# Interleaving the end of each superblock and splitting the first x load in a fused convolution and two-matmul kernel

## The chip, the cores and the metric

One core of a Trainium2 chip. The metric is the device time of one execution in microseconds (us), the median of several. A profiled execution has a span from its first to its last instruction, 1.8 to 2.2 us shorter than its time. Lengths and starts below are read from one profiled execution of each kernel, times from several.

## The reference

A dynamic convolution: each of 32768 tokens (8 sequences of 4096) has 8 heads with 7 softmax weights each, and each head's 24 channels are the weighted sum of that token and the 6 before it. The result x (192 wide) goes through two matmuls with a shrinking function between them.

```python
w = softmax(weight_gen)                       # [B, S, 8 heads, 7 taps]
x_pad = concat([zeros(B, 6, 192), x], axis=1) # six "halo" rows in front
out = einsum('bshk,bskhg->bshg', w, windows_of_7(x_pad))
h = out.reshape(32768, 192) @ w_in            # 192 -> 2048
y = (h - tanh(h)) @ w_out                     # 2048 -> 192, float32
```

## The kernel before

Tokens are worked in 32 superblocks of 1024 (128 partitions of 8 tokens). Four engines form a pipeline over different superblocks:

- GpSimd (POOL) makes the 7 products x times weight of superblock n+2 (`even`, `odd`, `last`); a DMA adds half of them to the other half.
- TensorE (PE) transposes and sums the products of n+1 by matmuls against an identity (`pc`), in two pieces; ScalarE (ACT) copies them out as `convT`.
- TensorE makes the 16 f tiles of n (`ph`, 128 rows of w_in's 2048 columns each); ScalarE takes their tanh; VectorE (DVE) subtracts (`gt`).
- TensorE makes the 8 output blocks of n−1 (`obank`), ScalarE copies them out.

The kernel's use of PSUM (where its matmuls write) is three buffers of two banks, used in turn by f tiles and transpose pieces, and two output banks.

```python
psum_h = tile_pool(name="psum_h", bufs=3, space=PSUM)     # "ph" and "pc" in turn
obank = [psum_o.tile([P, 512], FP32, ...) for i in range(2)]

def gemm1(n, f):                    # one f tile
    ph = psum_h.tile([P, 2, HT], FP32, name="ph", tag="ph")
    ...                             # 6 matmuls of 512 columns, two row halves side by side
    last_act[0] = nc.scalar.activation(out=th[:], in_=ph_f, func=ACT.Tanh)
    last_sub[0] = nc.vector.tensor_sub(gt[:], ph_f, th[:])

def gemm2(i):                       # output block i, 16 steps of two matmuls
    for f in range(NFT):
        for r, n, j, po in ops: nc.tensor.matmul(po[:, 0:D], lhsT=g_of[n][f][...], rhs=w_out[...])
    ...
    last_act[0] = nc.scalar.activation(out=out_sb[:, j, :], in_=po[:, 0:D], func=ACT.Copy)

for n in range(NTOT):
    ...                             # loads of n + 3
    for p in range(J):              # J = 8
        gemm1(n, 2 * p)
        gemm1(n, 2 * p + 1)
        ...
        if n >= 1:
            gemm2((n - 1) * J + p)
        ...
        if n + 1 < NTOT:            # after block 6: both transpose pieces (n > 1)
            if p == (6 if n > 0 else 7): conv(n + 1, (0, 1))
            if p == (6 if n > 1 else 7): conv(n + 1, (2,))
        if p == 6 and n + 3 < NTOT:
            softmax_norm(n + 3)     # sum and reciprocal, VectorE
```

x is loaded with its halo, 14 rows per partition of which 8 are its own.

The softmax here doesn't subtract the row's maximum and nothing guards it: scores larger than these inputs give would overflow.

## Time and profile before

| | before |
|---|---|
| time | 770.2 us (770.0 to 770.4) |
| span of the profiled execution | 768.7 us |
| TensorE busy | 96% |
| first f tile starts | 20.73 us |
| superblock 0 (VectorE's), first f tile to first f tile | 23.41 us |
| superblocks 1 to 3, together | 74.0 us |
| superblocks 4 to 30, most of them, each | 22.63 us |

In the timeline a line is: start, busy time, engine, source line, operation, what it writes and reads, count; in brackets the idle time before it and what ended it. The ends of matmuls are modelled, so TensorE's row can look unbroken where it waits 0.2 us: compare starts with the length that the same group has elsewhere. In the waits, a row is the waiter, what it waited for, the sum in us, the number of times, the longest. The prediction below shows the lines.

### The profile page before, as it was taken

How to read it: one execution, taken by the hardware profiler on the slowest of the kernel's cores; microseconds unless marked ns; L12 is line 12 of the kernel's file. 1: busy time of each engine (PE TensorE's matmuls, PEld its weight loads, DVE VectorE, ACT ScalarE, POOL GpSimd, SP SyncE). 2: the span in 40 equal slices, each digit the busy share in tenths (PEclk: the TensorE clock that was granted, in tenths of full speed). 3: DMA queues.
4: the chain of work that ended last, by engine and by line, in shares of the span. 5: the costliest groups of instructions: out<-in, count | busy, mean ns of one | idle time of the engine just before them, and what ended most of it. 6: DMA issues, size and time to landing. Idle time of an engine off the chain costs nothing.

```text
span 768.7 us, 32330 instructions
## 1 busy us (share of the span) xinstructions
PE 736.7 (96%) x14784; PEld 583.1 (76%) x14784; DVE 652.9 (85%) x595; ACT 640.8 (83%) x865; POOL 695.2 (90%) x290
## 2 busy tenths in 40 slices
PE   2799999999999999999999999999999999999997
PEld 2377787777777777788777777777778777787777
DVE  5987888888898888889888888888888988888883
ACT  1777878888888888888888888888888888888883
POOL 5999999999999999999999999999999999999100
PEclk9999999999999999999999999999999999999999
DMA  7823776555677555577655557765556765542412
GB/s 209 184 81 87 182 181 150 118 145 147 169 182 174 131 129 148 150 180 182 164 123 133 150 160 182 180 128 137 143 150 172 182 181 115 125 142 72 98 43 84
DMA packets 25847, 111.37 MB, mean 145 GB/s; under 512 B 4800, under 2 KB 9456, under 8 KB 21624
## 3 DMA queue, kind: packets, MB, share of 16 engines
q1 hardware_dynamic: 14688, 76.95, 29.9%
q0 software_dynamic: 10816, 31.99, 25.8%
q8 instruction: 115, 1.88, 1.0%
q10 hardware_dynamic: 208, 0.39, 0.2%
q14 instruction: 20, 0.16, 0.1%
HBM read 54.49 MB, written 25.17 MB: 104 GB/s over the span
## 4 chain that ended last, share of the span: by engine, by line
PE 93%; DVE 2%; issue 1%; POOL 1%; DMA 1%; ACT 1%; SPq 0%; POOLq 0%
PE ph L257 43%; PE obank L289 43%; PE pc L233 6%; DVE gt L269 2%; PE po L323 1%; DMA x_t<-in_x_dram 1%; POOL even L192 1%; ACT th L267 0%; ACT convT L244 0%; POOL odd L192 0%; DVE zr L151 0%; DVE zsum L145 0%; SPq L117 0%; SPq L93 0%; SPq L121 0%
## 5 line engine op out<-in xcount | busy, mean ns | idle before, releaser
L269 DVE TENSOR_TENSOR gt<-ph,th 128x1024 bf16<-128x1024 f32 x512 | 602.8, 1219 | 93.3 <-ACT th L267 92.7
L267 ACT ACTIVATE th<-ph 128x1024 f32<-128x1024 f32 x512 | 497.2, 1022 | 65.7 <-PE ph L257 64.9
L257 PE MATMUL ph<-convT,w_in 64*128 64x512 bf16 x3072 | 382.1, 378 | 7.5 <-DVE gt L269 5.0
L289 PEld LDWEIGHTS <-gt 64*128 64x128 bf16 x7936 | 345.1, 94 | 53.4 <-issue 2.5
L289 PE MATMUL obank<-w_out,gt 64*128 64x192 bf16 x7936 | 374.6, 243 | 2.9 <-issue 2.1
L192 POOL TENSOR_TENSOR even<-x_t,wsm 128x1536 bf16<-128x1536 f32 x94 | 272.8, 2903 | 3.9 <-DMA x_t<-in_x_dram 1.6
L192 POOL TENSOR_TENSOR odd<-x_t,wsm 128x1536 bf16<-128x1536 f32 x93 | 269.9, 2903 | 0.0
L257 PEld LDWEIGHTS <-w_in 64*128 64x128 bf16 x3072 | 180.1, 94 | 108.4 <-issue 11.8
L192 POOL TENSOR_TENSOR last<-x_t,wsm 128x1536 bf16<-128x1536 f32 x31 | 103.4, 3336 | 0.0
L307 ACT ACTIVATE out_sb<-obank 128x192 f32<-128x192 f32 x248 | 81.9, 330 | 10.5 <-PE obank L289 4.6
L244 ACT ACTIVATE convT<-pc 128x1024 bf16<-128x1024 f32 x64 | 48.9, 808 | 31.6 <-PE pc L233 31.5
L233 PE MATMUL pc<-ident,even 64*128 64x64 bf16 x2304 | 47.9, 192 | 2.9 <-POOL even L192 1.5
L233 PEld LDWEIGHTS <-even 64*128 64x128 bf16 x2304 | 42.7, 96 | 4.1 <-issue 2.2
L201 POOL DMA_DIRECT2D even<-odd x29 | 34.9, 1205 | 9.1 <-POOL odd L192 9.1
L163 POOL TENSOR_TENSOR wsm<-e_t,zr 128x448 f32<-128x448 f32 x30 | 41.7, 1390 | 0.0
L233 PE MATMUL pc<-ident,odd 64*128 64x64 bf16 x448 | 15.5, 198 | 13.1 <-DVE odd L192 12.8
L135 ACT ACTIVATE e_t<-wg_t 128x448 f32<-128x448 f32 x32 | 18.5, 578 | 8.2 <-DMA wg_t<-in_weight_gen_dram 8.2
L233 PE MATMUL pc<-ident,last 64*128 64x64 bf16 x768 | 23.3, 192 | 1.8 <-issue 1.7
L145 DVE TENSOR_REDUCE zsum<-e_t 128x64 f32<-128x448 f32 x32 | 19.5, 609 | 2.9 <-ACT e_t L135 2.9
L233 PEld LDWEIGHTS <-odd 64*128 64x128 bf16 x448 | 11.3, 100 | 13.6 <-DVE odd L192 12.9
L151 DVE RECIPROCAL zr<-zsum 128x64 f32<-128x64 f32 x30 | 16.6, 553 | 3.0
L233 PEld LDWEIGHTS <-last 64*128 64x128 bf16 x768 | 17.0, 96 | 2.2 <-issue 1.8
(20 smaller groups left out, 48.7 us busy)
## 6 DMA issues: line engine op xcount, KB each, us to landing
x_t<-in_x_dram SPq DMA_DIRECT2D x24, 1344.0 KB
even<-odd POOLq DMA_DIRECT2D x29, 1024.0 KB, 8.8
out_dram<-out_sb SPq DMA_DIRECT2D x31, 768.0 KB
x_t<-in_x_dram SPq DMA_DIRECT2D x8, 1176.0 KB
wg_t<-in_weight_gen_dram SPq DMA_DIRECT2D x32, 224.0 KB
x_t<-in_x_dram SPq DMA_DIRECT2D x8, 157.5 KB
w_in<-in_moe_w_in_dram POOLq DMA_DIRECT2D x6, 128.0 KB, 7.5
w_out<-in_moe_w_out_dram POOLq DMA_DIRECT2D x1, 768.0 KB, 10.8
```

What stands on the lines that cost most here:

```text
L135: nc.scalar.activation(out=e_t[:].rearrange("p j h k -> p (j h k)"), in_=wg_t[:].rearrange("p j h k -> p (j h k)"), func=ACT.Exp,)
L145: nc.vector.reduce_sum(out=zsum[:], in_=e_t[:].rearrange("p j h k -> p (j h) k"), axis=AX.X)
L163: return eng.tensor_mul(wsm.rearrange("p j h k -> p (j h) k"), e_t[:].rearrange("p j h k -> p (j h) k"), zr.rearrange("p (n o) -> p n o", ...
L192: eng.tensor_mul(dst[k].rearrange("p c j h g -> p j h c g"), x_t[:, k : k + J, :].rearrange("p j (h c g) -> p j h c g", h=H, c=NC), w[:, : ...
L201: nc.gpsimd.dma_start(out=even[:].rearrange("p i c j h g -> p (i c j h g)")[:, 0:ACC], in_=odd[:].rearrange("p i c j h g -> p (i c j h g)" ...
L233: nc.tensor.matmul(pc[:, r, col : col + R], lhsT=prods[c][gi][r * R : (r + 1) * R, c, 2 * j : 2 * j + 2].rearrange("p j h g -> p (j h g)") ...
L244: nc.scalar.activation(out=convT[:, c0 : c0 + nch, :].rearrange("p c (j r t) -> p r (c j) t", r=2, t=R), in_=pc[:, :, 0 : nch * JH * R].re ...
L257: nc.tensor.matmul(ph[:, r, :], lhsT=w_in[r * R : (r + 1) * R, c, f * P : (f + 1) * P], rhs=convT[r * R : (r + 1) * R, c, :], start=(c == ...
L267: last_act[0] = nc.scalar.activation(out=th[:], in_=ph_f, func=ACT.Tanh)
L269: last_sub[0] = nc.vector.tensor_sub(gt[:], ph_f, th[:])
L289: mm = nc.tensor.matmul(po[:, 0:D], lhsT=g_of[n][f][r * R : (r + 1) * R, col : col + P], rhs=w_out[r * R : (r + 1) * R, f, :], start=(r == ...
L307: last_act[0] = nc.scalar.activation(out=out_sb[:, j, :], in_=po[:, 0:D], func=ACT.Copy)
```

## The change

Its intent: spread the ends of superblocks so that TensorE alternates between kinds of work while ScalarE and VectorE catch up, and start the first products on the part of x that needs no halo.

```diff
-        if s == 0:
+        if n == 0:
+            rows(0, P, HALO, HALO + J)      # first tile: own rows, all partitions
+            rows(16, P, 0, HALO)            # then the halo
+            rows(1, 16, 0, HALO)
+            no_halo()
+        elif s == 0:
 ...
-    FA = 8 * P                              # first part of w_in
+    FA = 7 * P
 ...
     products(
         0,
-        on_vector=(3, 4, 5, 6),
-        sums=(3, 0, 4, 5, 1, 6, 2),
+        on_vector=(6, 3, 4, 5),
+        order_of=(6, 0, 3, 1, 4, 5, 2),
+        sums=(6, 3, 0, 4, 5, 1, 2),
 ...
+        spread = 1 < n < NTOT - 1
-        for p in range(J):
+        for p in range(J - 1 if spread else J):
 ...                                         # (superblock 1: pieces after blocks 5 and 6)
+        if spread:
+            (pc,) = conv_sums(n + 1, (0, 1))
+            conv_out(n + 1, pc, (0, 1), 0, 1)
+            if n + 3 < NTOT:
+                softmax_norm(n + 3)
+            gemm1(n, NFT - 2)
+            conv_out(n + 1, pc, (0, 1), 1, 1)
+            gemm2((n - 1) * J + J - 1, 0)   # steps 0 to 7 of the block
+            (pc,) = conv_sums(n + 1, (2,))
+            conv_out(n + 1, pc, (2,))
+            gemm2((n - 1) * J + J - 1, 1)   # steps 8 to 15
+            gemm1(n, NFT - 1)
```

The lines are shortened ("..."), with comments added. The rest of the diff splits `conv` into `conv_sums` and `conv_out` and lets `gemm2` run by halves.

More of the change, by code (lines that the diff above doesn't have):

```diff
@@ L103, in load_x, with rows @@
         x_t = xpool.tile([P, HALO + J, D], FP32, name="x_t")
-        def rows(p0, p1):
-            win = x[b, s0 + p0 * J - HALO : s0 + p0 * J - HALO + 1]
+        def rows(p0, p1, r0=0, r1=HALO + J):
+            win = x[b, s0 + p0 * J - HALO + r0 : s0 + p0 * J - HALO + r0 + 1]
             nc.sync.dma_start(
-                out=x_t[p0:p1, :, :],
+                out=x_t[p0:p1, r0:r1, :],
                 in_=bass.AP(
@@ L111, in rows, with no_halo @@
                     offset=win.offset,
-                    ap=[[J * D, p1 - p0], [D, HALO + J], [1, D]],
+                    ap=[[J * D, p1 - p0], [D, r1 - r0], [1, D]],
                 ),
             )
-        if s == 0:
+        def no_halo():
             nc.sync.dma_start(
@@ L120, in load_x @@
             )
-            nc.sync.dma_start(
-                out=x_t[0:1, HALO : HALO + J, :],
-                in_=x[b, 0:J].rearrange("(p j) d -> p j d", p=1),
-            )
+        if n == 0:
[4 more added lines that the diff above has]
+        elif s == 0:
+            no_halo()
+            rows(0, 1, HALO, HALO + J)
             rows(1, 16)
@@ L167, in scale, with products @@
         )
-    def products(n, on_vector=(), sums=None, hooks={}, behind=None):
+    def products(n, on_vector=(), order_of=None, sums=None, hooks={}, behind=None):
         x_t = x_of.pop(n)
@@ L189, in products @@
             hooks[-1]()
-        for k in range(K):
+        for k in order_of or range(K):
             eng, w = (nc.vector, wsm_v) if k in on_vector else (nc.gpsimd, wsm[:])
@@ L215, in products, with conv_sums @@
             prods_of[n] = [[dst[k] for k in (sums or range(K))]] * NC
-    def conv(n, *parts):
+    def conv_sums(n, *parts):
         prods = prods_of[n]
@@ L221, in conv @@
             conv_of[n] = cpool.tile([P, NC, HT], BF16, name="convT")
-        convT = conv_of[n]
         pcs = [psum_h.tile([P, 2, HT], FP32, name="pc", tag="ph") for _ in parts]
@@ L241, in conv, with conv_out @@
                             )
-        for chunks, pc in zip(parts, pcs):
-            c0, nch = chunks[0], len(chunks)
-            nc.scalar.activation(
-                out=convT[:, c0 : c0 + nch, :].rearrange("p c (j r t) -> p r (c j) t", r=2, t=R),
-                in_=pc[:, :, 0 : nch * JH * R].rearrange("p r (cj t) -> p r cj t", t=R),
-                func=ACT.Copy,
-            )
         if parts[-1][-1] == NC - 1:
             prods_of.pop(n)
+        return pcs
+    def conv_out(n, pc, chunks, c0=None, nch=None):
+        c0 = chunks[0] if c0 is None else c0
+        nch = len(chunks) if nch is None else nch
+        col = (c0 - chunks[0]) * HT // 2
+        nc.scalar.activation(
+            out=conv_of[n][:, c0 : c0 + nch, :].rearrange("p c (j r t) -> p r (c j) t", r=2, t=R),
+            in_=pc[:, :, col : col + nch * JH * R].rearrange("p r (cj t) -> p r cj t", t=R),
+            func=ACT.Copy,
+        )
+    def conv(n, *parts):
+        for pc, chunks in zip(conv_sums(n, *parts), parts):
+            conv_out(n, pc, chunks)
     def gemm1(n, f):
@@ L266, in gemm1 @@
         g1_act[0] = last_act.get(0)
+        gt = gpool.tile([P, TOK], BF16, name=f"gt{f}", tag=f"gt{f}")
         last_act[0] = nc.scalar.activation(out=th[:], in_=ph_f, func=ACT.Tanh)
-        gt = gpool.tile([P, TOK], BF16, name=f"gt{f}", tag=f"gt{f}")
         last_sub[0] = nc.vector.tensor_sub(gt[:], ph_f, th[:])
@@ L274, with gemm2 @@
     out_of = {}
-    def gemm2(i):
+    def gemm2(i, half_of=None):
         ops = []
@@ L282, in gemm2 @@
             n, j = divmod(blk, J)
-            if r == 0:
+            if r == 0 and half_of != 1:
                 half[blk] = obank[blk % 2]
             ops.append((r, n, j, half[blk]))
-        for f in range(NFT):
+        f0, f1 = (0, NFT) if half_of is None else (half_of * J, half_of * J + J)
+        for f in range(f0, f1):
             for r, n, j, po in ops:
@@ L299, in gemm2 @@
                     order(mm, g1_act[0] if i == 1 else last_act[0], "row tiles in one bank")
-        if i > 0:
+        if i > 0 and half_of != 0:
             blk = i - 1
@@ L360, in load_w_in @@
                 in_=bass.AP(
-                    tensor=src.tensor, offset=src.offset, ap=[[G * F, H], [F, GC], [1, f1 - f0]]
+                    tensor=src.tensor,
+                    offset=src.offset,
+                    ap=[[G * F, H], [F, GC], [1, f1 - f0]],
                 ),
@@ L409 @@
                 products(n + 2, behind=last_sub[0] if n > 1 else None)
-            if n + 1 < NTOT:
-                if p == (6 if n > 0 else 7):
-                    conv(n + 1, (0, 1))
-                if p == (6 if n > 1 else 7):
-                    conv(n + 1, (2,))
+            if n == 0 and p == 7:
+                conv(1, (0, 1))
+                conv(1, (2,))
+            if n == 1 and p == 5:
+                conv(2, (0, 1))
+            if n == 1 and p == 6:
+                conv(2, (2,))
             if n == 0 and p == 2:
@@ L417 @@
                 products(2)
-            if p == 6 and n + 3 < NTOT:
+            if n <= 1 and p == 6:
                 softmax_norm(n + 3)
+        if spread:
[10 more added lines that the diff above has]
+            gemm1(n, NFT - 1)
     gemm2(LAST)
```

## The prediction

> **What bounds the kernel now.** I read the page's busy shares first, then the chain of waits, then the timeline of one late superblock (a block of 1024 tokens; there are 32), because a share of busy time is an average and the change touches only the ends of superblocks and the first load. TensorE is at 96%, and the chain is TensorE almost throughout:
>
> ```profile
> PE 736.7 (96%) x14784; PEld 583.1 (76%) x14784; DVE 652.9 (85%) x595; ACT 640.8 (83%) x865; POOL 695.2 (90%) x290
> ...
> PE 93%; DVE 2%; issue 1%; POOL 1%; DMA 1%; ACT 1%; SPq 0%; POOLq 0%
> ```
>
> So only TensorE's own instruction time or a gap in it can move the total. The timeline around the end of superblock 24 (first superblock = 0) shows both:
>
> ```profile
> 590.61 2.36 DVE L269 TENSOR_TENSOR gt<-ph,th 128x1024 bf16<-128x1024 f32 x2 [0.26 <-ACT th L267]
> ...
> 591.31 0.88 PE L233 MATMUL pc<-ident,even 64*128 64x64 bf16 x48
> ...
> 592.01 0.41 PE L233 MATMUL pc<-ident,last 64*128 64x64 bf16 x16
> ...
> 592.24 0.53 PE L233 MATMUL pc<-ident,even 64*128 64x64 bf16 x24
> ...
> 592.46 1.51 ACT L244 ACTIVATE convT<-pc 128x1024 bf16<-128x1024 f32 x2 [0.60 <-PE pc L233]
> ...
> 592.71 0.30 PE L233 MATMUL pc<-ident,odd 64*128 64x64 bf16 x8
> ...
> 593.02 1.47 PE L257 MATMUL ph<-convT,w_in 64*128 64x512 bf16 x12
> ...
> 593.88 1.94 ACT L267 ACTIVATE th<-ph 128x1024 f32<-128x1024 f32 x2
> ...
> 594.31 1.50 PE L289 MATMUL obank<-w_out,gt 64*128 64x192 bf16 x32
> ...
> 594.94 2.36 DVE L269 TENSOR_TENSOR gt<-ph,th 128x1024 bf16<-128x1024 f32 x2 [0.79 <-ACT th L267]
> ...
> 595.63 1.48 PE L257 MATMUL ph<-convT,w_in 64*128 64x512 bf16 x12
> ```
>
> Read the starts, not the modelled ends. A pair of f tiles takes 594.31 − 593.02 = 1.295 us (0.648 a tile), an output block 1.32, the pair of both 2.615. The transposes take 592.01 − 591.31 = 0.70 us for 48, so 14.7 ns each, and all 104 should take 1.53. But the next f tile starts 1.71 after them. The 0.18 us in between is a hidden wait: f tile 14 takes the buffer of tile 13 (three PSUM buffers in turn, two of them taken by the transpose pieces). DVE's pair starts at 590.61 and the second of the two ends at 592.97, and 593.02 is 0.05 later. A superblock is 8 × 2.615 + 1.71 = 22.63 us, and the starts of the late superblocks are 22.62 to 22.64 apart.
>
> TensorE's other gaps between 44 and 753 us, in the view of waits:
>
> ```profile
> PE pc L233 <- issue: 2.8, 5, 1.7
> PE obank L289 <- issue: 2.1, 2, 1.3
> PE ph L257 <- issue: 0.8, 1, 0.8
> ```
>
> They are 5.7 us without a releaser, most of it near transposes in superblocks 1 to 3 and 20. Each of the four largest ends 1.3 to 1.6 us after one 16 KB packet of the instruction queue ended, so I read them as late instruction fetch; that is an inference. The head, in the timeline:
>
> ```profile
> 6.84 1.92 POOL L358 DMA_DIRECT2D w_in<-in_moe_w_in_dram  x3 [5.53 <-DVE wsm L163]
> 10.28 1.75 DVE L192 TENSOR_TENSOR odd<-x_t,obank 128x1536 bf16<-128x1536 f32 x1 [3.77 <-DMA x_t<-in_x_dram]
> 10.32 2.90 POOL L192 TENSOR_TENSOR even<-x_t,wsm 128x1536 bf16<-128x1536 f32 x1 [1.57 <-DMA x_t<-in_x_dram]
> ...
> 16.05 2.89 POOL L192 TENSOR_TENSOR even<-x_t,wsm 128x1536 bf16<-128x1536 f32 x1
> ...
> 20.73 4.85 PE L257 MATMUL ph<-convT,w_in 64*128 64x512 bf16 x24 [0.91 <-ACT convT L244]
> 20.85 3.39 PEld L257 LDWEIGHTS <-w_in 64*128 64x128 bf16 x18 [1.14 <-DMA w_in<-w_in]
> ```
>
> The weights are ready at 6.5, x comes only at 10.3; the first f tile waits for the transposes (which wait for GpSimd's third product, 16.05 + 2.89 = 18.94) and, at nearly the same moment, for the copy of w_in.
>
> [...]
>
> **The change part by part.**
>
> *TensorE's order at the end of superblocks 2 to 30.* No matmul is added or removed. Before: transposes (two pieces), tiles 14, 15, block. After: piece 1, tile 14, half a block, piece 2, other half, tile 15, and then the next superblock's tiles 0 and 1 directly. Durations, besides those above: piece 1 is 64 matmuls, 0.94 us, piece 2 is 40, 0.59, half a block 0.66. Latencies: f tile start to tanh 0.86 (593.88 − 593.02); tanh to its subtraction 1.05 when DVE is free (596.50 to 597.55); tanh to tanh 0.92; subtraction to subtraction 1.13 when queued (superblock 0); subtraction 1.22, and the buffer is refilled 0.05 after it (13 of 13 such tiles of superblock 0). Copy of one chunk 0.60, next ScalarE start 0.50 later; block end to its output copy 0.22. Time 0 is the start of piece 1; buffers in turn A (12), B (13), C (piece 1), A (14), B (piece 2), C (15), A (0'), B (1'), C (2'), A (3').
>
> - Tile 14 runs 0.94 to 1.59 and no longer waits for 13: the 0.18 is saved. Half block to 2.25, piece 2 to 2.84, half block to 3.50.
> - ScalarE: first copy 1.15, tanh 14 at 1.80, second copy 2.72 to 3.32, third 3.22, output 3.72. C is free at 3.37, so tile 15 runs 3.50 to 4.15: just in time.
> - DVE: subtraction 13 ends 1.65, the softmax pair at 2.84, subtraction 14 2.85 to 4.07. A is free at 4.12, tile 0' runs 4.15 to 4.80: just in time. 1' to 5.44.
> - tanh 15 at 3.50 + 0.86 = 4.36, subtraction 15 at 5.41 to 6.63. Subtraction 0' follows at 6.54 and ends 7.76.
> - The next block needs tile 15 in its last weight loads, near 6.5 to 6.7: about 0.1 late, ends 6.86. Tile 2' to 7.51. Tile 3' needs A: 7.76 + 0.05 = 7.81. It starts 0.30 late.
>
> Counted from tile 15: TensorE has three tiles, a block and one tile before 3', 4 × 0.648 + 1.32 = 3.91 us, while the chain to 3' is 0.86 + 1.05 + 1.13 + 1.22 + 0.05 = 4.31. So 0.40 us of new wait, whichever of the two places shows it, against 0.18 saved: +0.22 a superblock, 22.85 instead of 22.63. Over 29 superblocks: +6.4 us. ScalarE's third copy (0.3 us more) lies in its slack.
>
> *Superblock 1.* Piece 1 moves one pair earlier; GpSimd's products for it end at 57.24, before it. I put +0.1.
>
> *Head.* Main x is 128 × 6144 B = 0.79 MB of 1.38 MB. Before, x flowed from about 3.4 to 9.4 us, some 228 GB/s. The main transfer is now issued at about 1.2, ahead of the zero row's 0.83 us issue, and should serve VectorE's tap 6 (the product for the 7th and last filter position, which reads no halo row) at about 7.1. But taps 3 and 0 need the halo; the bytes are the same, so these start only as much earlier as the transfer does: 9.6 instead of 10.3. GpSimd still does three taps (8.6 us) and ends at about 18.2; VectorE gains more, but nothing waits for that. w_in's first part is 7/8 as large, so its copy, 18.4 to 20.5 before, is ready at about 19.8. First f tile 0.8 us earlier. The second part of w_in is larger and needed one tile sooner: it may stall tile 7 by a microsecond, yet DVE's softmax pair at 30.5 to 31.7 lies there and hides it. Superblock 0 is DVE's (16 subtractions at 1.13 and two softmax pairs), so the 0.8 is kept.
>
> *Instruction gaps.* The transposes, the densest stretch of instructions, are spread, but 252 of them still pass in 2.84 us. The loads that share the DMA engines in superblocks 1 to 3 remain. I allow −1.5 of 5.7.
>
> Sum: −0.8 + 0.1 + 6.4 − 1.5 = +4.2, from 770.2 to 774.4. The wait of 0.40 is read from margins of 0.03 to 0.13 us, and a late tile 0' would overlap it, not add; so I shade to 773.
>
> **The rivals.** (1) The order works as intended: no wait replaces the 0.18, the instruction gaps go. Then −5.2 − 5 − 1, about 759. For it: three of the waits come out just in time in my table; against it: the 4.31 us chain is made of durations that barely vary. GpSimd would also limit it: its own period is 22.64 to 22.65 us, with 7 us of slack at the last transposes (its last add lands at 720.3, they start at 727.1). (2) The margins fail: ScalarE's second copy delays tile 15 and subtraction 14 delays 0', by another 0.3 us each superblock; about 782. (3) The order is neutral, the saved wait equals the new one, and only the head and some gaps show: 768. (4) The second part of w_in comes later than the softmax pair hides: +1, the head's gain gone: 774.
>
> **Range and chances.** 2% is 15.4 us. Rival 1, the best case, is short of that, rival 2 as well. So 773, 8 in 10 within 765 to 782; faster by over 2%: 0.01, within 2%: 0.96, slower by over 2%: 0.03.
>
> **What would show it.** Late superblocks 22.85 us apart (right) or 22.45 to 22.65 (rival 1). Tile 14 right behind piece 1, 0.94 us after it began; the second pair's second tile of a superblock starting 0.05 us after the end of subtraction 0', about 0.3 late. VectorE's first product at 7.1, GpSimd's at 9.6, the first f tile at 19.9. The step most likely wrong is the 0.40, then the instruction gaps, which I can't derive.

The instruction queue carried 115 packets and 1.88 MB, 16 KB each, by the page of the kernel before.

## The result

| | before | after |
|---|---|---|
| time, median of 4 | 770.24 us | 774.38 us (773.71 to 774.72) |
| span of the profiled execution | 768.73 | 772.52 |
| first f tile starts | 20.73 | 19.18 |
| superblock 0 | 23.41 | 23.30 |
| superblock 1 | 25.55 | 28.70 |
| superblocks 2 and 3, together | 48.47 | 46.45 |
| superblocks 4 to 30, the most common length | 22.63 | 22.85 |
| superblocks 4 to 30, together | 613.25 | 617.14 |

The ratio is 1.0053, with a 95% interval of 1.0036 to 1.0070. A ratio is the mean time of one kernel's fast runs over that of the other's of the same rounds, so not quite the ratio of the medians quoted.

Timeline after, around the end of superblock 24:

```profile
593.53 0.88 PE L237 MATMUL pc<-ident,even 64*128 64x64 bf16 x48
...
594.47 0.83 PE L270 MATMUL ph<-convT,w_in 64*128 64x512 bf16 x6
...
597.02 2.12 PE L270 MATMUL ph<-convT,w_in 64*128 64x512 bf16 x18
...
597.88 2.86 ACT L281 ACTIVATE th<-ph 128x1024 f32<-128x1024 f32 x3 [0.32 <-PE ph L270]
...
598.94 4.62 DVE L282 TENSOR_TENSOR gt<-ph,th 128x1024 bf16<-128x1024 f32 x4 [1.32 <-ACT th L281]
...
598.96 1.52 PE L303 MATMUL obank<-w_out,gt 64*128 64x192 bf16 x32
...
600.32 0.81 PE L270 MATMUL ph<-convT,w_in 64*128 64x512 bf16 x6
...
601.35 0.82 PE L270 MATMUL ph<-convT,w_in 64*128 64x512 bf16 x6 [0.22 <-DVE gt L282]
```

Tile 14 starts at 594.47, 0.94 us after piece 1 and right behind it: the old wait of 0.18 is gone. The x18 group is tiles 15, 0' and 1' in a row. Tile 2' starts at 600.32 and tile 3' should start 0.65 later, at 600.97; it starts at 601.35, 0.38 late, released by a subtraction. The block before it takes 1.36 instead of 1.32. Together that is the new wait, 0.42 us. The waits of TensorE (44 to 752 us, the first two rows of four) show it 29 times:

```profile
PE ph L270 <- DVE gt L282: 6.5, 29, 0.2
PE pc L237 <- issue: 3.3, 2, 2.8
```

The 0.2 is the visible part; the rest lies under the modelled matmul ends. The second row, waits with no releaser in the profile, has the largest single gap of either kernel:

```profile
66.49 0.24 PE L237 MATMUL pc<-ident,odd 64*128 64x64 bf16 x5 [2.76 <-issue]
```

It is in superblock 1, and the clock then falls. Busy time and granted clock after, by stretch (PEclk, the third number from the end, is the share of full TensorE speed):

```profile
60.00:67.70 7.70, 4.94 (x156) 4.21 (x150) 4.01 (x5) 3.66 (x5) 7.70 (x3) 1.00 0.52 147
67.70:71.10 3.40, 3.40 (x39) 2.74 (x35) 2.28 (x2) 2.06 (x3) 3.40 (x3) 0.50 0.00 0
...
```

From 67.71 us, 1.2 us after the gap, TensorE ran at half clock (PEclk 0.50) for 3.41 us, by estimate (half of 3.41) 1.7 us lost. In end_alternate, below, a gap of 2.87 us in the same superblock, ending at 67.28 us, was not followed by it (PEclk 1.00 in all three stretches from 60 to 75 us), so the length of the gap alone does not decide; what does was not shown. It seems not to come in every execution: of the four timed ones, that with a mean granted clock of 1.000 took 773.71 us, the others (0.997 to 0.998) 774.19 to 774.72.

The head after, in the timeline:

```profile
6.44 1.75 DVE L197 TENSOR_TENSOR last<-x_t,obank 128x1536 bf16<-128x1536 f32 x1
6.84 1.92 POOL L372 DMA_DIRECT2D w_in<-in_moe_w_in_dram  x3 [5.53 <-DVE wsm L168]
...
8.39 1.75 DVE L197 TENSOR_TENSOR odd<-x_t,obank 128x1536 bf16<-128x1536 f32 x1 [0.21 <-DMA x_t<-zero]
...
8.76 2.94 POOL L197 TENSOR_TENSOR even<-x_t,wsm 128x1536 bf16<-128x1536 f32 x1
...
19.18 4.80 PE L270 MATMUL ph<-convT,w_in 64*128 64x512 bf16 x24 [0.90 <-ACT convT L255]
```

VectorE's first product no longer waits for x at all. GpSimd starts at 8.76 instead of 10.32 and the first f tile at 19.18 instead of 20.73, 1.55 us earlier as well. GpSimd does not wait for x any more either: VectorE already works on rows with halo at 8.39, and 8.76 is when GpSimd's own issuing of the w_in loads ends (6.84 + 1.92).

### The profile page after: what moved, and what is told of

It reads as the page before. It is cut to its first block, busy times and chain, and to the rows that moved or that the text cites. A ratio compares the mean times of both kernels' runs of the same rounds, so it can differ in the third digit from the quotient of the medians.

```text
span 772.5 us, 32358 instructions
## 1 busy us (share of the span) xinstructions
PE 738.7 (96%) x14784; PEld 572.8 (74%) x14784; DVE 650.3 (84%) x595; ACT 642.9 (83%) x894; POOL 696.2 (90%) x290
## 3 DMA queue, kind: packets, MB, share of 16 engines
q8 instruction: 115, 1.88, 1.0%
## 4 chain that ended last, share of the span: by engine, by line
PE 81%; DVE 9%; ACT 4%; issue 4%; POOL 1%; DMA 0%; DVEq 0%
PE obank L303 38%; PE ph L270 36%; DVE gt L282 8%; PE pc L237 6%; ACT th L281 4%; PE po L337 1%; POOL even L197 1%; DMA wg_t<-in_weight_gen_dram 0%; DVE zsum L150 0%; POOL w_in L372 0%; DVE zr L156 0%; ACT convT L255 0%; DVE obank L168 0%; DVE wsm L168 0%; DVEq L282 0%
## 5 line engine op out<-in xcount | busy, mean ns | idle before, releaser
L270 PE MATMUL ph<-convT,w_in 64*128 64x512 bf16 x3072 | 386.4, 378 | 12.3 <-DVE gt L282 11.1
L303 PE MATMUL obank<-w_out,gt 64*128 64x192 bf16 x7936 | 381.2, 243 | 1.0 <-ACT out_sb L321 0.4
L270 PEld LDWEIGHTS <-w_in 64*128 64x128 bf16 x3072 | 170.3, 94 | 123.2 <-issue 25.6
L255 ACT ACTIVATE convT<-pc 128x512 bf16<-128x512 f32 (+1 forms) x93 | 53.5, 613 | 32.9 <-PE pc L237 32.9
L168 POOL TENSOR_TENSOR wsm<-e_t,zr 128x448 f32<-128x448 f32 x30 | 32.5, 1082 | 2.8 <-DVE gt L282 2.7
```

The source lines that it names most:

```text
L168: return eng.tensor_mul(wsm.rearrange("p j h k -> p (j h) k"), e_t[:].rearrange("p j h k -> p (j h) k"), zr.rearrange("p (n o) -> p n o", ...
L255: nc.scalar.activation(out=conv_of[n][:, c0 : c0 + nch, :].rearrange("p c (j r t) -> p r (c j) t", r=2, t=R), in_=pc[:, :, col : col + nch ...
L270: nc.tensor.matmul(ph[:, r, :], lhsT=w_in[r * R : (r + 1) * R, c, f * P : (f + 1) * P], rhs=convT[r * R : (r + 1) * R, c, :], start=(c == ...
L303: mm = nc.tensor.matmul(po[:, 0:D], lhsT=g_of[n][f][r * R : (r + 1) * R, col : col + P], rhs=w_out[r * R : (r + 1) * R, f, :], start=(r == ...
```

## The experiments

The theory: the new order loses 0.40 us per superblock because tile 3' needs the PSUM buffer of tile 0', whose tanh and subtraction queue behind those of tile 15; it saves the old 0.18; the new head gains; and the gaps without a releaser are a separate matter. Rivals: the new loads disturb the early superblocks; the extra ScalarE copy, or the softmax pair on VectorE, is the cost; any alternation is. Each kernel was timed in five rounds unless said otherwise, beside the kernel before (770.16 to 770.64 us in these rounds). "Length" is the most common distance between the first f tiles of superblocks 4 to 30. All results are correct except where said.

**order_only**: the changed kernel with the x load, the products of tile 0 and `FA` of before.

> The head of before with the new order of superblock ends. Theory (a new wait of 0.40 us on the PSUM buffer of tile 0' against 0.18 us saved): superblocks 4 to 30 start 22.85 us apart as in the changed kernel, first f tile at 20.7 as before; total 774.4 + 1.6 = 776.0, give or take 1.5 for instruction gaps in superblocks 1 to 3. Rival (the loss belongs to the new loads, which disturb the early superblocks): about 770.

Measured: 775.74 us (ratio 1.0075, 1.0062 to 1.0088), length 22.85. First f tile 20.36.

**head_only**: the new head with the loop of before.

> The new head with the old loop. Theory: first f tile at 19.2, late superblocks 22.63 apart, 770.2 - 1.6 = 768.6, give or take 1.5. Rival: 772 to 774.

Measured: 769.23 us (ratio 0.9987, 0.9973 to 1.0000, so the gain is barely clear of the noise), length 22.63, first f tile 19.32. The head comes out 1.4 us earlier, but gaps without a releaser ate part: superblocks 1 to 3 take 74.4 instead of 74.0 and 4 to 30 take 614.2 instead of 613.3. So the order costs 5.6 us, the head gains 0.9, and their sum, 4.7, is near the 4.1 of both. The rival of the loads falls.

**tile15_ahead**

```diff
+            gemm1(n, NFT - 1)
             gemm2((n - 1) * J + J - 1, 1)
-            gemm1(n, NFT - 1)
```

> The changed kernel with tile 15 before the second half block instead of behind it. Theory: the wait behind tile 0' vanishes (0.66 us of other work lies between tile 15 and tile 3'), but tile 15 now waits for the copy of piece 1, from 2.84 to 3.37 us after the start of piece 1, 0.53 us: superblocks 22.98 apart, TensorE's wait moves from DVE gt to ACT convT, 774.4 + 29 x 0.13 = 778.2. Rival (the wait of 0.40 is the softmax pair or the longer ScalarE work, not the distance from tile 15 to tile 3'): 22.85 or more with the wait still on DVE gt.

Measured: 778.33 us (1.0106, 1.0092 to 1.0120), length 22.97. The four runs are 777.1, 777.3, 779.3 and 779.4; the profiled one is of the slower pair, and in it x arrived late and the first f tile started at 21.27, which is not this edit's doing. Compare the lengths. The waits of TensorE, and two lines of the timeline:

```profile
PE ph L270 <- ACT convT L255: 10.3, 29, 0.4
PE pc L237 <- issue: 3.2, 2, 2.9
```

```profile
599.74 0.53 PE L237 MATMUL pc<-ident,even 64*128 64x64 bf16 x24
...
600.86 0.82 PE L270 MATMUL ph<-convT,w_in 64*128 64x512 bf16 x6 [0.36 <-ACT convT L255]
```

No row for DVE gt is left (the one row not shown is an output block that waits once for a tanh); the wait is now for the copy of piece 1. In the timeline tile 15 starts 1.12 us after piece 2, which takes 0.58: 0.54 late. The wait at tile 3' is removed by nothing but 0.66 us of other work between tile 15 and tile 3'. This is the distance theory's result; the softmax pair and ScalarE's total are unchanged. In the changed kernel VectorE also sat idle for 1.32 us before tile 15's subtraction (the line at 598.94), so the softmax pair is not what delays it.

**two_of_16_after**

```diff
-            gemm2((n - 1) * J + J - 1, 1)                  # 1: steps J to NFT - 1
+            gemm2((n - 1) * J + J - 1, (J, NFT - 2))
             gemm1(n, NFT - 1)
+            gemm2((n - 1) * J + J - 1, (NFT - 2, NFT))
```

> The changed kernel with the last two of the block's 16 steps (0.165 us) moved behind tile 15. Theory: 3' waits 0.23 instead of 0.40 and tile 15 waits 0.03 for piece 1's copy: superblocks 22.72 apart, 774.4 - 29 x 0.135 = 770.5. Rival: no change, 774.4.

Measured: 771.09 us (1.0013, 1.0001 to 1.0026), length 22.73. Two steps moved, 0.165 us of distance, and each superblock gained 0.12.

**copy_unsplit**

```diff
-            conv_out(n + 1, pc, (0, 1), 0, 1)
+            conv_out(n + 1, pc, (0, 1))
 ...
-            conv_out(n + 1, pc, (0, 1), 1, 1)
```

> The changed kernel with piece 1 copied by one ScalarE instruction of 1.02 us instead of two of 0.60. Theory: tanh 14 starts at 2.07 instead of 1.80, subtraction 14 ends 0.27 later, so tile 0' waits 0.24 us, and tile 3' then only 0.15: the chain from tile 15 to tile 3' is untouched, so the superblocks stay 22.85 apart and the total at 774.4; the split by itself buys nothing here. Rival (the third copy's 0.3 us of ScalarE is what costs): 22.6 apart, 767.

Measured: 774.45 us (1.0057, 1.0043 to 1.0071), length 22.85. Timeline, the same place:

```profile
596.80 2.39 PE L270 MATMUL ph<-convT,w_in 64*128 64x512 bf16 x18
599.01 1.50 PE L303 MATMUL obank<-w_out,gt 64*128 64x192 bf16 x32
600.33 1.62 PE L270 MATMUL ph<-convT,w_in 64*128 64x512 bf16 x12
601.77 1.42 PE L303 MATMUL obank<-w_out,gt 64*128 64x192 bf16 x30
```

The three tiles take 599.01 − 596.80 = 2.21 instead of 1.94, the pair 1.44 instead of 1.30: waits of 0.26 and 0.15 in two places, and the same length. The third copy's instruction cost nothing, and the split earned nothing (774.38 us with it, 774.45 without): it removes a wait that the later one would have covered.

**sb1_old_places**

```diff
-            if n == 1 and p == 5:            # piece 1
+            if n == 1 and p == 6:
-            if n == 1 and p == 6:            # piece 2
+            if n == 1 and p == 7:
```

> The changed kernel with superblock 1's two pieces back at the places of before (after blocks 6 and 7 instead of 5 and 6). Theory: the gap of 2.8 us in superblock 1 and the half clock after it come from the dense transposes meeting the load of x at 58 to 63 us; later places meet it less: superblock 1 25.5 instead of 28.7, total 771.5. Rival[...]: 774 or so, with the gap elsewhere.

Measured: 774.47 us (1.0057, 1.0043 to 1.0071). A miss. Superblock 1 does take 25.2 instead of 28.7, without the half clock (mean granted clock 1.000), but superblock 2 takes 24.8 instead of 22.8 and superblock 3 24.3 instead of 23.7. Most of the time in gaps moved to the next superblocks (the three together 74.2 instead of 75.2), as the rival had it.

**alternate_all**: from superblock 2 on, tile, half a block, tile, half a block throughout (the diff is condensed).

```diff
             gemm1(n, 2 * p)
+            if spread: gemm2(blk, (0, J))
 ...                                         # last pair: piece 2 first, piece 1 here
             gemm1(n, 2 * p + 1)
+            if spread: gemm2(blk, (J, NFT))
```

> A candidate: from superblock 2 on, one f tile, half a block, one f tile, half a block throughout, piece 2 first and piece 1 in the middle of the last pair, copied whole. Theory: the distance from a tile to the third tile after it is 3 x 0.648 + 3 x 0.66 = 3.92 us at least, over the chain of 3.18, and no wait is left: TensorE needs 22.45 a superblock; GpSimd's 22.65 and its last add at about 719 then bound it: 760 to 766, with transposes waiting for GpSimd or the add near the end. Rival (each switch between kinds of matmul costs TensorE something): over 770.

Measured: 821.56 us (1.0667, 1.0653 to 1.0680), length 24.58. A clear miss. Its timeline and waits:

```profile
590.30 0.83 PE L270 MATMUL ph<-convT,w_in 64*128 64x512 bf16 x6
...
590.77 0.32 ACT L320 ACTIVATE out_sb<-obank 128x192 f32<-128x192 f32 x1
...
591.15 0.84 PE L302 MATMUL obank<-w_out,gt 64*128 64x192 bf16 x16
```

```profile
PE obank L302 <- ACT out_sb L320: 21.5, 55, 0.5
```

I had looked at the three f-tile buffers only. The next block needs the other output bank, and ScalarE copies that out behind the tanh of the tile that now comes last before it. The copy ends at 591.09; the half block, due 0.65 after 590.30 at 590.95, starts at 591.15. In superblock 24 that is 0.20 us in five of the 8 pairs, 0.47 in the first, 0.67 in the one where the softmax's exponential lies ahead, and none in the last, 2.1 in all: the 24.58 less 22.45. A PSUM wait again, in the other pool.

**end_alternate**: only the last pair alternates, in an order that keeps all the distances.

```diff
-            (pc,) = conv_sums(n + 1, (0, 1))
-            conv_out(n + 1, pc, (0, 1), 0, 1)
-            if n + 3 < NTOT:
-                softmax_norm(n + 3)
+            (pc,) = conv_sums(n + 1, (2,), done=False)
+            conv_out(n + 1, pc, (2,))
             gemm1(n, NFT - 2)
-            conv_out(n + 1, pc, (0, 1), 1, 1)
             gemm2((n - 1) * J + J - 1, 0)
-            (pc,) = conv_sums(n + 1, (2,))
-            conv_out(n + 1, pc, (2,))
-            gemm2((n - 1) * J + J - 1, 1)
+            if n + 3 < NTOT:
+                softmax_norm(n + 3)
+            (pc,) = conv_sums(n + 1, (0, 1), done=True)
+            conv_out(n + 1, pc, (0, 1))
             gemm1(n, NFT - 1)
+            gemm2((n - 1) * J + J - 1, 1)
```

> Only the last pair of a superblock alternates, as in the changed kernel, but piece 2 first, then tile 14, half a block, piece 1 (copied whole), tile 15, half a block; the softmax pair behind subtraction 14; pairs elsewhere, so each output copy is early enough for the two output banks. Theory: from tile 15 to tile 3' TensorE has 4 x 0.648 + 0.66 + 1.32 = 4.57 us of work against the chain of 4.31, tile 14 takes tile 12's buffer, and the other margins are 0.02 to 0.3: superblocks 22.45 to 22.5 apart, 774.4 - 29 x 0.36 = 764, give or take 2 for instruction gaps; GpSimd's add of the last products (near 719) leaves a floor near 762. Rival (any alternation costs, by the output banks or ScalarE as in the run that alternated everywhere): 774 or more.

Measured: 767.03 us (766.49 to 768.05; ratio 0.9947, 0.9934 to 0.9961). It beats both kernels. The shortest superblocks are 22.46 and the most common length is 22.47, as the theory has it, and no wait for DVE gt on f tiles is left. But it is 3 us over the expected 764 and just outside its margin: superblocks 4 to 30 take 611.9, 5.2 us more than 27 × 22.47. Summing where TensorE's groups last longer than usual gives 5.0 us in 19 places, nearly all transposes or the tile after them, each with a 16 KB packet of the instruction queue that ended 1.3 to 1.6 us before TensorE went on. The changed kernel has 0.1 us of this in the same superblocks. Measured as what superblocks 4 to 30 take over 27 times the common length, such time is 5.2 us here, 2.2 in the kernel before and 3.2 in head_only (a PSUM wait of 0.18 in each superblock), and 0.1 to 1.3 in the runs with a longer PSUM wait. So roughly it grew where the wait shrank; why is not shown.

**no_x_loads** (three rounds; wrong result): end_alternate, but from tile 3 on the x of tiles 1 and 2 is used again.

```diff
+        if n >= 3:
+            x_of[n] = kept[n % 2]
+            return
         x_t = xpool.tile([P, HALO + J, D], FP32, name="x_t")
+        kept[n % 2] = x_t
```

> Wrong result on purpose: the end_alternate kernel, but from superblock 3's tile on the x of tiles 1 and 2 is used again instead of a load of 1.34 MB per superblock. Theory (the remaining TensorE gaps, 2.9 us in superblock 1 and about 5 us over superblocks 4 to 30[...]): the gaps nearly vanish, superblocks at 22.47 throughout, about 760, if GpSimd's products, at 22.65 a superblock, don't hold the last transposes. Rival[...]: the gaps stay where the dense transposes are, about 767.

What the run puts to the test is whether the loads of x cause the gaps; by what means they would was inference.

Measured: 761.51 us (ratio 0.9885, 0.9869 to 0.9902). TensorE's waits from 44 to 752 us, first of end_alternate (less two rows of output blocks that wait for ScalarE), then all of this kernel:

```profile
PE pc L237 <- issue: 4.2, 5, 2.9
PE ph L270 <- issue: 0.5, 2, 0.3
...
PE obank L303 <- issue: 0.4, 1, 0.4
```

```profile
PE pc L242 <- DMA even<-odd: 1.2, 1, 1.2
PE pc L242 <- DVE gt L287: 0.8, 2, 0.4
PE obank L308 <- ACT out_sb L326: 0.4, 1, 0.4
PE obank L308 <- ACT th L286: 0.4, 1, 0.4
PE ph L275 <- DVE gt L287: 0.3, 1, 0.3
```

Not one wait without a releaser is left. Superblocks 1 to 3 take 69.5 instead of 72.8. What remains in superblocks 4 to 30 are six pieces of transposes that wait for the add of GpSimd's products, now that TensorE runs ahead of GpSimd's 22.65 us: each starts 0.13 to 0.14 us after such an add has landed (two of them are the rows put down to DVE gt).

## Why the prediction was right

It gave 774.4 as the sum, shaded to 773; the median is 774.38. The order's share was right by its mechanism. That the sum agrees to 0.02 us is luck, because the errors of two other terms cancel in part. Point by point:

- **The new wait, 0.40 us.** Right: 0.42 in the trace (0.38 at tile 3', 0.04 in the block before), length 22.85, 29 times. Two runs varied the distance from tile 15 to tile 3' and the wait followed; one moved the wait to another place with the length unchanged, as the chain of latencies demands.
- **The old wait, 0.18.** Right: tile 14 follows piece 1 at once.
- **The two "just in time" margins** (tile 15 and tile 0') held, so the downward shading for an overlap was not called for.
- **The head, −0.8.** It had the direction right and half the size: −1.55 to the first f tile. Two steps failed. The first is x's rate: I took the 228 GB/s of the old transfer for the new ones. In the trace's DMA packets, tile 0's x ran from 3.4 to 9.5 us before and from 2.6 to 7.1 us after, the same bytes in 4.5 instead of 6.0 us, some 305 GB/s. Why it was faster is not shown, and it need not be the cut into own rows and halo: tile 1's x, 14 overlapping rows in both kernels, took 4.5 us before (9.4 to 13.9) and 4.2 after (7.2 to 11.4), 309 and 330 GB/s. The second is GpSimd's start: I let it wait for x until 9.6, but it starts at 8.76, held by its own issuing of w_in, so a still faster x would not have moved it. The feared stall of tile 7 for w_in was 0.2 us and, as foreseen, hidden behind VectorE: tile 8 follows tile 7 at VectorE's usual 1.13 us.
- **Gaps without a releaser, −1.5, and superblock 1, +0.1.** Together about −0.9: span +3.79 less 29 × 0.22 for the order and plus 1.66 for the head and superblock 0. The changed kernel has almost none after superblock 3, but the largest in superblock 1, and half the clock after it, so that superblock 1 alone took 3.15 more instead of 0.1. The error of this term has the opposite sign of the head's.
- **That these gaps are instruction fetch** was inference and is not shown. The run without x loads removes them all, so the load of x causes them. That it does so by delaying instruction packets fits the times (a packet ends 1.3 to 1.6 us before TensorE goes on; before the largest gap of the kernel before, the DMA engines are busy at a mean share of 0.97 or more from 103 to 113 us, and the packet starts at 112.4). But no run delayed a packet by itself, and the times alone prove little: in no_x_loads the six waits for an add also end 1.5 us after such a packet.
- **Rival 1**, no new wait, would have needed another order: end_alternate has its length of 22.45 to 22.5, but with more gaps without a releaser.

What stays open is why the gaps in superblocks 1 to 3 add up to about the same wherever the transposes of superblock 1 are.

## What to carry to other kernels

When an order is changed around buffers used in turn, add up two things for every reuse: the latency from the write of a buffer to its release, with the queue on each engine, and the work that the writer has between that write and the reuse. Do it for every pool: here three tiles in a row lost to one ring, alternating everywhere lost to the other, and of the new orders tried only the one that kept both distances won. With the same three buffers the order alone gave 22.97, 22.85, 22.63 or 22.47 us a superblock. A gain on the bounding engine also has to be checked against what comes up once its slack is gone, here gaps without a releaser and GpSimd's period (22.65 us).
